# Operands of the last rows: from the rows by parts, without the normalized copy in DRAM

## The chip, the cores and the metric

One core of a Trainium2 chip. The time is the device time of one execution, in microseconds; each kernel is run several times and the median stands for it. The profile is of one further execution, taken by the hardware profiler. TensorE is called PE, VectorE DVE, ScalarE ACT, GpSimd POOL; SP issues most of the DMAs, POOL the rest.

## The reference

A transformer block with conditioned layer norms, S = 2048 rows, D = 576, hidden size F = 4608, 32 heads of 18.

```
h = layernorm(x) * (1 + ca) + sa
x = x + ga * (softmax(q k^T / sqrt(18)) v) @ wo          # q, k, v from h @ wqkv
h = layernorm(x) * (1 + cb) + sb
x = x + gb * ((sigmoid(h @ w_gate) * (h @ w_up)) @ w_down)
```

`sa, ca, ga, sb, cb, gb` are the six parts of `silu(c) @ w_mod`. Everything is float32; the kernel multiplies in a reduced float32 (`F32R`) and carries a high and a low part of each operand, so that a product is three matmuls.

## The kernel before

The gated unit (the last line of the reference) is done in two halves of 1024 rows. For each half, the hidden size is worked through in 18 blocks of 256 columns. In a block the two products with `w_gate` and `w_up` are made by a scheme with seven products in place of eight (`ORDER` names them 1, 6, 2, 7, 5, 4, 3): operands and weights are cut in two by rows and columns, and sums and differences of the pieces are multiplied. `product` (the matmuls of L1031) does one of the seven, `gate` the sigmoid and the split into high and low parts `hh` and `hl`, and `down` (L1067) the product with `w_down` for four tiles of 128 rows, added to `Oa` by DVE at L1071. `down` runs twice a block, behind products 6 and 7 of the next block. It takes PSUM banks named `d`, of which there are three.

`weights_operand` prepares the weights of a product three products ahead (`LOOK`): sums `S` on POOL (L879), the high part `w` by a cast on ACT (L913), the low parts on DVE and POOL (L918). In the first half each is also stored in DRAM (`ws`) for the second.

The seven operands of the rows lie in DRAM (`xs`), high and low parts, and are loaded into SBUF for a half as a whole. Those of the first 1024 rows are made during attention. Those of the last 1024 rows are made during the first half of the gated unit, by the generator `last_rows`: the main loop calls one of its steps at every second product. Its three stages before the change:

- Eight steps with matmuls finish the attention's output projection for each tile of 128 rows and store the row tile in DRAM (`x1d`, L1156).
- For each of two groups of four tiles, the rows are loaded again (`z<-x1d`), their mean and variance taken (`ln_stats`), normalized (`ln_rows`, L686), and `ln_spill` transposes them on PE (L701), applies scale and bias on ACT while leaving PSUM (L1160) and stores them in DRAM (`hs`, L705).
- For each third `i` of the columns four blocks `B` are loaded from `hs` (L1190), and `operand_parts` makes the seven operands from them: differences of blocks on POOL (L728); then, for each of the seven, the high part by a cast on ACT (L717), the low part by a subtraction on POOL (L719; for the last third two narrow ones, L724), and a store to `xs` (L720, L725). High and low part share a tile `ho`, of which there are two.

In `operand_parts` the casts come in a fixed order: block 11, block 22, block 21, then block 22 again once POOL has taken block 12 from it, then the three others. A cast therefore waits for POOL, and the next use of a `ho` tile for the store of its last contents.

PE's order is written out by the program from the ninth block on (`ORDERED`). The order on the other engines and on SP's queue is set by a scheduler when the kernel is built, from its own estimates of durations. Each engine works strictly in its order.

Of the kernel before, what the change touches and what calls it, by code (L numbers as in the profile page):

```python
# [23 lines left out]
P = 128  # L24
S = 2048
# [26 lines left out]
def tile_block(ctx, tc, x_in, wqkv, wo, w_gate, w_up, w_down, c_in, w_mod, out):  # L52
# [95 lines left out]
    def ln_stats(pool, xt, mv):  # L148
        st = pool.tile([P, 2, nc.vector.BN_STATS_DIM], F32, name="st", bufs=2)
        for g in range(2):  # L150
            nc.vector.bn_stats(st[:, g, :], xt[:, g, :] if len(xt.shape) == 3 else xt[:, g * HALF : (g + 1) * HALF])
        nc.vector.bn_aggr(mv, st)

    def ln_scales(pool, mv, rs):
        for _ in ln_scales_steps(pool, mv, rs):
            pass
# [72 lines left out]
        return got  # L229

    gates = dram.tile([2, D], F32, name="gates")
    hs = dram.tile([2, 3, P, S], F32, name="hs")
    x1d = dram.tile([P, 8, D], F32, name="x1d")
    x1p = dram.tile([P, 8, D], F32, name="x1p")
    oend = dram.tile([P, 8, D - DL], F32, name="oend")
# [444 lines left out]
        if t >= 8:  # L680
            nc.gpsimd.dma_start(x1p[:, t - 8, :], xt)

    def ln_rows(z, t, x1, eng):

        zx = z[:, :, 0:HALF]
        eng.tensor_scalar(  # L686
            zx, x1, mv2[:, t, 0:1], rs2[:, t : t + 1], op0=ALU.subtract, op1=ALU.mult
        )
        nc.gpsimd.tensor_copy(
            z[:, :, HALF:384].rearrange("p g (r c) -> p g r c", c=32),  # L690
            z[:, :, HALF - 32 : HALF].unsqueeze(2).to_broadcast([P, 2, 3, 32]),
        )

    def ln_spill(zs, ch, psum, pool, put):


        for g in range(2):
            for i in range(3):
                pt = psum()
                for j, z in enumerate(zs):  # L700
                    nc.tensor.transpose(pt[:, j * P : (j + 1) * P], z[:, g, i * P : (i + 1) * P], ident)  # L701
                ev = pool.tile([P, 512], F32, name="ev", bufs=2)
                c = 3 * g + i
                put(ev, pt, mcol2[:, 0, c : c + 1], mcol2[:, 1, c : c + 1])
                nc.sync.dma_start(hs[g, i, :, ch * 512 : (ch + 1) * 512], ev)  # L705
                yield

    def operand_parts(half, i, blocks, parts, hi, lo_eng, queue):


# [166 lines left out]
    def put(eng, to, a, b, op):  # L877
        for v in range(2):
            eng.tensor_tensor(to[:, v], a[:, v], b[:, v], op=op)  # L879
# [233 lines left out]
    def last_rows():  # L1113


        def psum():
            return pd.tile([P, 512], F32, name="d")

        with tc.tile_pool(name="fin", bufs=1, side="right") as pool:
            w = pool.tile([P, 2, 2, D], F32R, name="w")  # L1120
            nc.gpsimd.dma_start(w, wod)
            for t0 in (0, 4):
                od = pool.tile([P, 4, 256], F32, name="od")
                nc.sync.dma_start(od[:, :, 0:192], oend[:, t0 : t0 + 4, :])
# [12 lines left out]
                om = pool.tile([P, 512], F32R, name="om")  # L1137
                omh = pool.tile([P, 512], F32R, name="omh")
                nc.vector.tensor_copy(om[0:64], pt[0:64])
                nc.vector.tensor_copy(omh[64:P], pt[64:P])  # L1140
                nc.vector.tensor_sub(om[64:P], pt[64:P], omh[64:P].bitcast(F32))
                yield
                for j in range(4):
                    rows = slice(j * P, (j + 1) * P)
                    xt = pool.tile([P, D], F32, name="xt", bufs=2)
                    nc.sync.dma_start(xt, x1p[:, t0 + j, :])
                    for h in range(2):
                        cols = slice(h * HALF, (h + 1) * HALF)
# [10 lines left out]
        def modulated(ev, pt, scale, bias):  # L1159
            nc.scalar.activation(ev, pt, AF.Identity, scale=scale, bias=bias)  # L1160

        with tc.tile_pool(name="zp2", bufs=1, side="right") as zp:
            for ch in (2, 3):
                zs = []
                for t in range(4 * ch, 4 * ch + 4):
                    z = zp.tile([P, 2, 384], F32, name="z", bufs=4)
                    x1 = z[:, :, 0:HALF]
                    for g in range(2):
                        nc.sync.dma_start(z[:, g, 0:HALF], x1d[:, t - 8, g * HALF : (g + 1) * HALF])
                    ln_stats(zp, x1, mv2[:, t, :])  # L1170
                    zs.append(z)
                four = slice(4 * ch, 4 * ch + 4)
                ln_scales(zp, mv2[:, four, :], rs2[:, four])
                for j, z in enumerate(zs):
# [3 lines left out]
        with tc.tile_pool(name="xop2", bufs=2) as pool:  # L1178

            def get():  # L1180
                return [pool.tile([P, 512], F32, name="B", bufs=5) for _ in range(5)]

            def parts():
                return pool.tile([P, 2, 512], F32R, name="ho")

            for i in range(3):
                blocks = get()
                for (g, r), t in zip(((0, 0), (0, 1), (1, 0), (1, 1)), blocks):
                    cols = slice(HW + r * 512, HW + (r + 1) * 512)
# [96 lines left out]
```

## Time and profile before

| | |
|---|---|
| median of 3 runs | 2920.76 us (2920.69 to 2922.99) |
| the profiled execution | 2920.71 us |
| its span, first to last instruction | 2918.9 us |
| PE busy | 2855.8 us, 98% of the span |
| DVE, ACT, POOL busy | 73%, 55%, 28% |
| the chain that ended last, by engine | PE 89%, DMA 3%, ACT 3%, DVE 2%, POOL 2% |

How the lines are read. A line of a group is: source line, engine, operation, output<-inputs, partitions x elements and type, count, then busy time and mean ns of one, then the engine's idle time just before them and who ended most of it. A line of the timeline begins with the start and the length in microseconds, and ends, where the engine was idle before, with that idle time and who ended it. In a line on waits, `ACT ho L717 <- DMA xs<-ho: 39.9, 12, 6.7` says that ACT, before the instruction of L717 that writes `ho`, waited 39.9 us in 12 cases, the longest 6.7, for a DMA from `ho` to `xs`. The granted clock is a share of PE's full speed.

### The profile page before, as it was taken

The page shows a single profiled execution, that of the slowest core. Times are in us where ns is not written, and L with a number is a line of the kernel's source. Part 1 is how long each engine was busy: PE and PEld are TensorE (multiplying, and loading weights), DVE is VectorE, ACT ScalarE, POOL GpSimd, SP SyncE. Part 2 cuts the span into 40 slices and gives each one's busy share as a digit, 9 for nine tenths or more (in the row PEclk, how much of TensorE's full clock was granted, in tenths as well). Part 3 has the DMA queues.
Part 4 walks back from the last instruction along what each step waited for, and adds up shares of the span by engine and source line. Part 5 has one row for each costly group of instructions (what it writes and reads, how often), then busy time and mean ns, then how long its engine had stood idle before and what let it go on. Part 6 is the DMA issues. An engine that isn't in the chain of part 4 may idle for free.

```text
span 2918.9 us, 46640 instructions
## 1 busy us (share of the span) xinstructions
PE 2855.8 (98%) x17141; PEld 1880.8 (64%) x17141; DVE 2135.0 (73%) x3896; ACT 1614.4 (55%) x3022; POOL 814.1 (28%) x972
## 2 busy tenths in 40 slices
PE   7999999999999999999999999988999999999999
PEld 5874333343334443443443888877888888888888
DVE  7567888888888888998882777756777555555555
ACT  3227889999998888999888333333333111111111
POOL 3102014444213111661103544467543100000000
PEclk9999999999999999999999999999999999999999
DMA  5344123333212110221125866676666844444443
GB/s 176 115 147 145 49 76 131 122 125 123 90 49 77 34 53 21 99 95 63 50 86 185 289 220 234 232 250 237 225 211 238 300 167 169 167 168 167 159 159 137
DMA packets 137261, 425.97 MB, mean 146 GB/s; under 512 B 18884, under 2 KB 56520, under 8 KB 124744
## 3 DMA queue, kind: packets, MB, share of 16 engines
q1 hardware_dynamic: 121272, 342.42, 34.7%
q0 software_dynamic: 15760, 80.56, 7.8%
q8 instruction: 135, 2.21, 0.3%
q14 instruction: 94, 0.77, 0.1%
HBM read 264.45 MB, written 157.95 MB: 145 GB/s over the span
## 4 chain that ended last, share of the span: by engine, by line
PE 89%; DMA 3%; ACT 3%; DVE 2%; POOL 2%; issue 1%; SPq 1%; POOLq 0%; ACTq 0%; DVEq 0%
PE o L537 17%; PE x L1031 14%; PE d L1067 14%; PE s L959 13%; PE s L446 11%; PE bg L1031 5%; PE bu L1031 5%; PE s L294 3%; PE s L334 2%; PE s L676 2%; ACT p L963 2%; DMA xs<-ho 1%; DMA B<-hs 1%; PE s L561 1%; ACT oT L551 1%
## 5 line engine op out<-in xcount | busy, mean ns | idle before, releaser
L963 ACT ACTIVATE p<-s 128x512 f32<-128x512 f32 x2048 | 1068.5, 608 | 141.2 <-PE s L446 91.8
L459 DVE TENSOR_REDUCE mx<-s 128x1 f32<-128x512 f32 x1568 | 1015.4, 685 | 142.2 <-PE s L446 128.2
L446 PE MATMUL s<-k,q 54*128 54x512 f32 x1920 | 649.2, 439 | 2.1 <-ACT p L963 1.6
L959 PE MATMUL s<-q,k 56*128 56x512 f32 x1920 | 578.5, 433 | 2.7
L959 PEld LDWEIGHTS s<-q,k 56*128 56x128 f32 x1920 | 274.5, 185 | 472.2 <-ACT p L963 304.0
L537 PE MATMUL o<-p,vaug 128*32 128x512 f32 x4096 | 555.0, 607 | 0.0
L1067 PE MATMUL d<-wd,hh 128*128 128x288 f32 x2304 | 469.4, 298 | 20.9 <-DVE Oa L1071 20.7
L1067 PEld LDWEIGHTS d<-wd,hh 128*128 128x128 f32 x2304 | 379.0, 191 | 29.9 <-DVE Oa L1071 24.4
L1071 DVE TENSOR_TENSOR Oa<-Oa,d 128x288 f32<-128x288 f32 x576 | 257.8, 452 | 151.4 <-PE d L1067 147.8
L446 PEld LDWEIGHTS s<-k,q 54*128 54x128 f32 x1920 | 308.1, 185 | 69.2 <-ACT p L963 38.5
L1067 PE MATMUL d<-wd,hl 128*128 128x288 f32 x1152 | 343.7, 298 | 0.1
L1031 PE MATMUL x<-k,w 128*128 128x512 f32 x994 | 238.3, 390 | 0.5 <-DVE u L1245 0.5
L1043 ACT ACTIVATE u<-u 128x512 f32<-128x512 f32 x72 | 45.5, 632 | 328.9 <-DVE u L1233 310.3
L1067 PEld LDWEIGHTS d<-wd,hl 128*128 128x128 f32 x1152 | 219.7, 191 | 0.3 <-DVE hl L1047 0.3
L1031 PEld LDWEIGHTS x<-k,w 128*128 128x128 f32 x994 | 184.1, 188 | 37.5 <-DVE u L1245 0.9
L537 PEld LDWEIGHTS o<-p,vaug 128*32 128x32 f32 x4096 | 83.5, 108 | 164.7 <-issue 149.2
L1040 ACT ACTIVATE sg<-x 128x512 f32<-128x512 f32 x36 | 21.5, 598 | 285.1 <-PE x L1031 285.1
L1073 POOL DMA_DIRECT2D out_dram<-Oa x16 | 8.7, 544 | 606.4 <-DVE Oa L1071 606.4
L454 DVE CUSTOM_DVE_ANT_0 rise<-s,rise 128x512 f32<-128x512 f32 x240 | 163.4, 681 | 0.0
L452 ACT ACTIVATE rise<-s 128x512 f32<-128x512 f32 x240 | 151.4, 631 | 0.0
L918 POOL TENSOR_TENSOR w<-S,w 64x256 fp32r<-64x256 f32 x69 | 72.2, 1046 | 212.9 <-ACT w L913 202.4
L1031 PE MATMUL x<-w,w 128*128 128x512 f32 x504 | 123.5, 395 | 0.0
(240 smaller groups left out, 3772.7 us busy)
## 6 DMA issues: line engine op xcount, KB each, us to landing
w<-ws SPq DMA_DIRECT2D x126, 640.0 KB
ws<-w SPq DMA_DIRECT2D x124, 640.0 KB
wd<-wds SPq DMA_DIRECT2D x36, 1152.0 KB
wds<-w POOLq DMA_DIRECT2D x18, 1152.0 KB, 4.5
k<-kd SPq DMA_DIRECT2D x30, 360.0 KB
w<-in_B_w_down_dram POOLq DMA_DIRECT2D x18, 576.0 KB, 5.0
q<-qd SPq DMA_DIRECT2D x64, 144.0 KB
raw<-in_B_w_gate_dram SPq DMA_DIRECT2D x34, 256.0 KB
```

The lines of the kernel that those rows point to most:

```text
L294: nc.tensor.matmul(acc, w, hT[:, t, cols], start=n == 0, stop=n == len(ts_) - 1)
L446: nc.tensor.matmul(sp, qs[rows, qt * P : (qt + 1) * P], ks[rows, kc * 512 : (kc + 1) * 512], start=True, stop=True,)
L452: nc.scalar.activation(rise, sp, AF.Relu)
L454: nc.vector.tensor_tensor_reduce(rise, sp, rise, 1.0, -3.0e38, ALU.add, ALU.max, mx[0][:, qt, 0:1])
L459: nc.vector.tensor_reduce(mx[h][:, qt, j : j + 1], sp, axis=AX.X, op=ALU.max)
L537: nc.tensor.matmul(acc[32 * j : 32 * j + 32, :], vaug[:, kt, (2 * p + h) * VW : (2 * p + h) * VW + 32], probs[2 * c + h], start=kt == 0, s ...
L918: eng.tensor_sub(w[rows, :, to, :], src[rows, :, a, :], w[rows, :, a, :].bitcast(F32))
L959: nc.tensor.matmul(sT, ks[rows, kcols], qs[rows, c * 512 : (c + 1) * 512], start=True, stop=True)
L963: state["exp"] = nc.scalar.activation(pr, sT, AF.Exp, scale=SCALE)
L1031: nc.tensor.matmul(acc[v], w[:, v, a, :], X[s][:, b, :], start=first and n == 0, stop=n == 6, skip_group_check=not first,)
L1067: nc.tensor.matmul(acc[:, :HALF], a[:, f, rows], w[:, f, cols], start=n == 0, stop=n == 5)
L1071: nc.vector.tensor_add(Oa[:, t, cols], Oa[:, t, cols], acc[:, :HALF])
```

## The change

The copy `hs` in DRAM, `ln_rows` and `ln_spill` are removed. The statistics are taken from each row tile while it is still in SBUF, in the first stage. Then, for each of twelve parts (a third `i` of the columns, half `g` of them, four row tiles `r`), the 128 columns of four row tiles are loaded from `x1d` in one DMA (for the last third 32 columns), two parts ahead; DVE normalizes them, four pieces of 128x128; PE transposes them; and ACT applies scale and bias on leaving PSUM, straight into a block `B`. After four parts `operand_parts` runs on the blocks as before. Its stores are issued by POOL instead of SP, and `ho` has three tiles instead of two.

```
-    hs = dram.tile([2, 3, P, S], F32, name="hs")
...
                     nc.sync.dma_start(x1d[:, t0 + j, :], xt)
+                    ln_stats(pool, xt, mv2[:, 8 + t0 + j, :])
                     yield
...
-                    for g in range(2):
-                        nc.sync.dma_start(z[:, g, 0:HALF], x1d[:, t - 8, g * HALF : (g + 1) * HALF])
-                    ln_stats(zp, x1, mv2[:, t, :])
...
-                    ln_rows(z, 4 * ch + j, z[:, :, 0:HALF], nc.vector)
-                yield
-                yield from ln_spill(zs, ch, psum, zp, modulated)
...
-                return pool.tile([P, 2, 512], F32R, name="ho")
...
-                    nc.sync.dma_start(t, hs[g, i, :, cols])
-                yield from operand_parts(1, i, blocks, parts, nc.scalar.copy, nc.gpsimd, nc.sync)
+        with tc.tile_pool(name="xop2", bufs=1, side="right") as pool:
+            order = [(i, g, r) for i in range(3) for g in range(2) for r in range(2)]
+
+            def load_part(i, g, r):
+                z = pool.tile([P, 4, P], F32, name="z", bufs=4)
+                c0, n = g * HALF + i * P, P if i < 2 else 32
+                nc.sync.dma_start(z[:, :, 0:n], x1d[:, 4 * r : 4 * r + 4, c0 : c0 + n])
+                return z
+
+            def normalized_part(z, i, g, r):
+                to = z if i < 2 else pool.tile([P, 4, P], F32, name="z", bufs=4)
+                for j in range(4):
+                    t = 8 + 4 * r + j
...
+                    nc.vector.tensor_scalar(
+                        a, x, mv2[:, t, 0:1], rs2[:, t : t + 1], op0=ALU.subtract, op1=ALU.mult
+                    )
+                return to
+
+            def parts():
+                return pool.tile([P, 2, 512], F32R, name="ho", bufs=3)
+
+            ahead = [load_part(*order[0])]
+            for _ in ln_scales_steps(pool, mv2[:, 8:16, :], rs2[:, 8:16]):
                 yield
...
+            for n, (i, g, r) in enumerate(order):
+                pt = psum()
+                for j in range(4):
+                    nc.tensor.transpose(pt[:, j * P : (j + 1) * P], z[:, j, :], ident)
+                c = 3 * g + i
+                blocks.append(pool.tile([P, 512], F32, name="B", bufs=5))
+                nc.scalar.activation(
+                    blocks[-1], pt, AF.Identity,
+                    scale=mcol2[:, 0, c : c + 1], bias=mcol2[:, 1, c : c + 1],
+                )
+                if n + 2 < len(order):
+                    ahead.append(load_part(*order[n + 2]))
+                if n + 1 < len(order):
+                    z = normalized_part(ahead.pop(0), *order[n + 1])
+                yield
+                if g and r:
+                    blocks.append(pool.tile([P, 512], F32, name="B", bufs=5))
+                    yield from operand_parts(1, i, blocks, parts, nc.scalar.copy, nc.gpsimd, nc.gpsimd)
+                    blocks = []
```

How it moves instructions. The names are the program's; `w<-raw` and `w<-S` are the weights' casts, `sg` the first sigmoid of a block, `hh` the high part of a gate's result, `p` a copy of the first product. Lines of the changed kernel that stand for lines of the one before: L691 for L717 (the operand casts), L693 and L698 for L719 and L724, L694 and L699 for L720 and L725, L702 for L728, L887 for L913, L892 for L918, L853 for L879, L1014 for L1040, L1020 for L1046, L1173 for L1160.

On ACT, where the first set of operand casts began before:

```order
L913 CAST w<-S_23872 128x2x384
L913 CAST w<-raw_23590 128x2x384
L717 CAST ho<-B 128x512 x3
L1040 ACTIVATE sg<-x 128x512
L913 CAST w<-S_23873 128x2x384
L717 CAST ho<-B 128x512
L1046 CAST hh_24099<-sg 128x512
L717 CAST ho<-B 128x512
L913 CAST w<-raw_23882 128x2x384
L717 CAST ho<-B 128x512
```

On ACT with the change, the first set from the fourth part's eviction on:

```order
L1173 ACTIVATE B<-d,mcol_74 128x512
L1020 CAST hh_22990<-u_23031 128x512
L691 CAST ho<-B 128x512 x2
L1017 ACTIVATE p_22865<-p_22865 128x512
L887 CAST w<-raw_22844 128x2x384
L1020 CAST hh_22988<-p_22865 128x512
L691 CAST ho<-B 128x512
L1017 ACTIVATE u_22902<-u_22902 128x512
L887 CAST w<-S_23208 128x2x384
L691 CAST ho<-B 128x512
L1205 COPY p_23236<-x 128x512
L1020 CAST hh_22990<-u_22902 128x512
```

and the third set, likewise:

```order
L1173 ACTIVATE B<-d,mcol_74 128x512
L1020 CAST hh_25107<-u_25019 128x512
L691 CAST ho<-B 128x512
L1205 COPY p_25354<-x 128x512
L691 CAST ho<-B 128x512
L1205 COPY p_25354<-x 128x512
L887 CAST w<-S_25258 128x2x384
L691 CAST ho<-B 128x512
L887 CAST w<-raw_24960 128x2x384
L691 CAST ho<-B 128x512 x3
L1014 ACTIVATE sg<-x 128x512
```

In the first set before, three casts of the six shown stand ahead of `sg`, behind the block's last `w<-raw`. With the change one cast of each set stands about a block earlier, and the six others between the fourth part's eviction and the next `sg`: in the first set all of them ahead of the last `w<-raw`, in the third set three ahead of it and three right behind. The three sets begin with their evictions in blocks 4, 7 and 11 (counted from 0) and end in blocks 6, 9 and 12.

On POOL, the last third before (the narrow subtractions):

```order
L724 TENSOR_TENSOR ho<-B,ho 32x512 x2
L918 TENSOR_TENSOR w<-S_24576,w 64x2x128
L879 TENSOR_TENSOR S_24925<-S_24924,raw_24585 128x384 x2
L728 TENSOR_TENSOR B<-B 128x512
L918 TENSOR_TENSOR w<-raw_24585,w 64x2x128
L728 TENSOR_TENSOR B<-B 128x512
L724 TENSOR_TENSOR ho<-B,ho 32x512 x2
L728 TENSOR_TENSOR B<-B 128x512
L724 TENSOR_TENSOR ho<-B,ho 32x512 x2
```

and with the change:

```order
L702 TENSOR_TENSOR B<-B 128x512
L853 TENSOR_TENSOR S_25671<-raw_25268 128x384
L702 TENSOR_TENSOR B<-B 128x512
L698 TENSOR_TENSOR ho<-B,ho 32x512 x3
L699 DMA xs<-ho 128x512
L702 TENSOR_TENSOR B<-B 128x512
L892 TENSOR_TENSOR w<-S_25258,w 64x2x128
L698 TENSOR_TENSOR ho<-B,ho 32x512
L853 TENSOR_TENSOR S_25604<-raw_25268,raw_25333 128x384 x2
L699 DMA xs<-ho 128x512
L853 TENSOR_TENSOR S_25671<-raw_25268 128x384
L892 TENSOR_TENSOR w<-raw_24960,w 64x2x128
```

The store's issue now stands on POOL between them, and the third difference (the one on which the fourth cast depends) behind three narrow subtractions and an issue.

More of the change, by code (lines that the diff above doesn't have):

```diff
@@ L681, in project_o @@
             nc.gpsimd.dma_start(x1p[:, t - 8, :], xt)
[L683 to L694, printed above, removed]
-        for g in range(2):
[L698 to L705, printed above, removed]
-                yield
     def operand_parts(half, i, blocks, parts, hi, lo_eng, queue):
@@ L1156, in last_rows @@
                     nc.sync.dma_start(x1d[:, t0 + j, :], xt)
+                    ln_stats(pool, xt, mv2[:, 8 + t0 + j, :])
                     yield
[L1159 to L1168, printed above, removed]
-                        nc.sync.dma_start(z[:, g, 0:HALF], x1d[:, t - 8, g * HALF : (g + 1) * HALF])
-                    ln_stats(zp, x1, mv2[:, t, :])
[L1171 to L1174, printed above, removed]
-                    ln_rows(z, 4 * ch + j, z[:, :, 0:HALF], nc.vector)
-                yield
-                yield from ln_spill(zs, ch, psum, zp, modulated)
@@ L1178, in last_rows @@
[L1178 to L1183, printed above, removed]
-                return pool.tile([P, 2, 512], F32R, name="ho")
[L1186 to L1189, printed above, removed]
-                    nc.sync.dma_start(t, hs[g, i, :, cols])
-                yield from operand_parts(1, i, blocks, parts, nc.scalar.copy, nc.gpsimd, nc.sync)
+        with tc.tile_pool(name="xop2", bufs=1, side="right") as pool:
[9 more added lines that the diff above has]
+                    t = 8 + 4 * r + j
+                    if i < 2:
+                        a, x = z[:, j, :], z[:, j, :]
+                    else:
+                        a = to[:, j, :].rearrange("p (n c) -> p n c", c=32)
+                        x = z[:, j, 0:32].unsqueeze(1).to_broadcast([P, 4, 32])
+                    nc.vector.tensor_scalar(
[6 more added lines that the diff above has]
+            for _ in ln_scales_steps(pool, mv2[:, 8:16, :], rs2[:, 8:16]):
+                yield
+            ahead.append(load_part(*order[1]))
+            yield
+            z = normalized_part(ahead.pop(0), *order[0])
+            blocks = []
[13 more added lines that the diff above has]
+                    z = normalized_part(ahead.pop(0), *order[n + 1])
+                yield
+                if g and r:
+                    blocks.append(pool.tile([P, 512], F32, name="B", bufs=5))
+                    yield from operand_parts(1, i, blocks, parts, nc.scalar.copy, nc.gpsimd, nc.gpsimd)
+                    blocks = []
```

## The prediction

> **What bounds the kernel now.** I read the page's busy times first, then the chain of waits in order of time, then TensorE's instructions where that chain leaves it.
>
> ```profile
> span 2918.9 us, 46640 instructions
> PE 2855.8 (98%) x17141; PEld 1880.8 (64%) x17141; DVE 2135.0 (73%) x3896; ACT 1614.4 (55%) x3022; POOL 814.1 (28%) x972
> ```
>
> PE is the bound: only what makes it wait or work can move the time. The change lies in the first half of the gated unit. There PE's own rows show each block's third product (seven products and two down steps make a block):
>
> ```profile
> 1903.99 3.35 PE L1031 MATMUL x<-w,w 128*128 128x512 f32 x14
> 1946.29 3.35 PE L1031 MATMUL x<-w,w 128*128 128x512 f32 x14
> 1995.43 3.35 PE L1031 MATMUL x<-w,w 128*128 128x512 f32 x14
> 2037.36 3.37 PE L1031 MATMUL x<-w,w 128*128 128x512 f32 x14
> 2072.37 3.35 PE L1031 MATMUL x<-w,w 128*128 128x512 f32 x14
> ```
>
> The last pair is a clean block: 35.0 us. The three blocks before it, in which the operands are built, took 133.4 where three clean ones take 105.0: **28.4 us are lost**, all of it without extra PE work. Where PE stood, its timeline says:
>
> ```profile
> 1914.14 0.53 PE L1067 MATMUL d<-wd,hh 128*128 128x288 f32 x2 [1.25 <-DVE Oa L1071]
> 1916.98 0.85 PE L1067 MATMUL d<-wd,hh 128*128 128x288 f32 x2 [1.78 <-DVE Oa L1071]
> 1960.79 0.85 PE L1067 MATMUL d<-wd,hh 128*128 128x288 f32 x2 [4.81 <-DVE Oa L1071]
> 1988.87 0.85 PE L1067 MATMUL d<-wd,hh 128*128 128x288 f32 x2 [4.70 <-DVE Oa L1071]
> 2031.68 0.64 PE L1067 MATMUL d<-wd,hh 128*128 128x288 f32 x2 [4.31 <-DVE Oa L1071]
> ```
>
> These are 16.9 us. PE waits for VectorE to empty a bank of the down product; VectorE was itself waiting for a cast on ScalarE; and ScalarE, which works in order, stood at the operand casts (the list of who waited for whom, 1690 to 2400 us: total, times, longest):
>
> ```profile
> ACT ho L717 <- DMA xs<-ho: 39.9, 12, 6.7
> ACT ho L717 <- DMA B<-hs: 18.8, 5, 6.6
> ```
>
> The other 11.5 us are the clock: after such a stall it is granted below full speed for some microseconds (0.77 in the stretch of the 4.70 stall; columns: stretch, length, PE, PEld, DVE, ACT, POOL busy, clock, DMA).
>
> ```profile
> 1980.00:1995.00 15.00, 10.24 (x52) 9.54 (x51) 9.54 (x16) 6.74 (x12) 11.78 (x11) 0.77 0.65 241
> ```
>
> **The change, part by part.** PE's work is the same: 48 transposes go and 48 come, in the same banks. The 12 evictions with scale and bias stay on ScalarE. Gone: 12 stores to and 12 loads from the DRAM copy, the wait for those loads (18.8 us of ScalarE's time), two table loads on ScalarE, eight 0.60 us copies on POOL. VectorE gets 48 pieces of 128x128 for 8 rows of 128x576; the 589 ns row bounds them above and the 199 ns of an almost empty VectorE instruction below; at 0.25 us it is 12 for 4.7 us over nine blocks, of which about 0.3 us stands before a bank's emptying in each set: under 1 us on the path.
>
> ```profile
> L689 POOL COPY z<-z 128x192 f32<-128x192 f32 x8 | 4.6, 602 | 14.8 <-DMA raw<-in_B_w_gate_dram 7.6 <-DVE z L686 7.0
> L686 DVE TENSOR_SCALAR z<-z,mv,rs 128x576 f32<-128x576 f32 x8 | 4.2, 589 | 0.1
> L152 DVE BATCH_NORM_AGGREGATE mv<-st 128x2 f32<-128x12 f32 x8 | 1.6, 199 | 0.0
> ```
>
> The loads of parts are two steps ahead, some 20 us before their transposes, so I cost them at nothing; without that cover each would stop PE for its landing.
>
> The 21 operand stores move from SP's queue to POOL's, and their tile has three buffers for two. On POOL such an issue costs 0.73 us (0.56 for a narrow one) and lands 3.2 to 5.2 us later; I take 4.0:
>
> ```profile
> L720 POOL DMA_DIRECT2D xs<-t x9: 727/727/807, 1176.2 to 1262.3; - x9
> L725 POOL DMA_DIRECT2D xs<-t x5: 543/560/633, 1291.0 to 1326.5; - x5
> xs<-t POOLq DMA_DIRECT2D x9, 512.0 KB, 3.2
> Oa<-x1d POOLq DMA_DIRECT2D x8, 288.0 KB, 5.2
> ```
>
> What decides is the order. Before, the 21 casts stand spread over five blocks. Now they stand in three sets: cast 1 early, casts 2 to 7 close together (in the third set all six ahead of the next `sg`). Cast 4 needs a subtraction on POOL that stands behind all earlier POOL work, and casts 5, 6 and 7 reuse the buffers of 2, 3 and 4, so they need those stores landed. POOL's prices:
>
> ```profile
> L719 POOL TENSOR_TENSOR ho<-B,ho 128x512 fp32r<-128x512 f32 x14 | 18.9, 1350 | 14.0 <-ACT ho L717 13.7
> L724 POOL TENSOR_TENSOR ho<-B,ho 32x512 fp32r<-32x512 f32 x14 | 19.7, 1407 | 1.6 <-ACT ho L717 0.7
> L728 POOL TENSOR_TENSOR B<-B 128x512 f32<-128x512 f32 x12 | 16.3, 1355 | 7.6 <-DMA B<-hs 7.0
> L879 POOL TENSOR_TENSOR S<-raw 128x384 f32<-128x384 f32 x28 | 35.8, 1299 | 12.7 <-DVE w L918 12.6
> L918 POOL TENSOR_TENSOR w<-S,w 64x256 fp32r<-64x256 f32 x60 | 62.1, 1035 | 191.0 <-ACT w L913 181.0 <-issue 7.5 <-POOL ho L719 0.5
> ```
>
> I lay each set over the clean block of the trace (ScalarE's and VectorE's rows of it):
>
> ```profile
> 2094.28 0.62 ACT L1046 CAST hh<-p 128x512 fp32r<-128x512 f32 x1 [1.17 <-DVE p L1044]
> 2096.57 0.82 ACT L913 CAST w<-S 128x768 fp32r<-128x768 f32 x1
> 2098.03 0.62 ACT L1046 CAST hh<-u 128x512 fp32r<-128x512 f32 x1 [0.64 <-DVE u L1044]
> 2101.24 0.84 ACT L913 CAST w<-raw 128x768 fp32r<-128x768 f32 x1 [0.89 <-POOL S L879]
> 2102.29 0.44 DVE L1071 TENSOR_TENSOR Oa<-Oa,d 128x288 f32<-128x288 f32 x1
> 2103.34 0.81 DVE L1071 TENSOR_TENSOR Oa<-Oa,d 128x288 f32<-128x288 f32 x2
> 2109.16 0.60 ACT L1040 ACTIVATE sg<-x 128x512 f32<-128x512 f32 x1 [7.08 <-PE x L1031]
> 2114.70 0.46 DVE L1071 TENSOR_TENSOR Oa<-Oa,d 128x288 f32<-128x288 f32 x1
> ```
>
> VectorE's second `Oa` stands behind the weights' subtraction, which needs the `w<-raw` cast; the `Oa` at 2114.70 stands behind `sg`. Whatever makes these casts late makes PE late, less about 0.6 us that the three banks cover.
>
> *Third set* (narrow parts). The fourth block is there at 2098.6. POOL then does subtraction, S, subtraction, three narrow ones, an issue, the subtraction for cast 4: 3 x 1.36 + 1.30 + 3 x 1.41 + 0.56 = 10.2, so cast 4 starts at 2108.8 and `w<-raw` at 2109.4, eight late. Up to the store that cast 7 needs, POOL has another w, narrow, S, S, issue, S, w, subtraction, three narrow, issue: 2 x 1.0 + 4 x 1.41 + 3 x 1.25 + 1.36 + 2 x 0.56 = 13.9, to 2122.7; landed at 2126.7; `sg` then starts at 2127.3 instead of 2109.2. Its product, the two weights' and `hl` pieces and two adds (3.9 us on VectorE) put the `Oa` at about 2131.7 instead of 2114.7: 17.0, less 0.6: **16.4 us**.
>
> *First set.* Fourth block at 2090.6 on POOL; subtraction twice, S, operand, S, issue, w, subtraction: 9.5; cast 4 at 2100.1 where ScalarE was free at 2096. Cast 6 waits for a store issued at 2102.2 (landed 2106.2), cast 7 for one issued at 2108.0 (2112.0). `w<-raw` ends at 2113.5, the second `Oa` at 2114.7 instead of 2103.8: 10.9, less 0.6: **10.3**.
>
> *Second set.* From 2094.9 on POOL: two subtractions, an operand, an issue (2099.7, landed 2103.7: cast 5), w, a subtraction (2102.1: cast 4), an operand, an issue (2104.2, landed 2108.2: cast 6). `w<-raw` ends at 2109.7, the second `Oa` at 2110.9: 7.1, less 0.6: **6.5**.
>
> Together 33.2 us of stalls. They make four stretches of reduced clock where now there are five for 11.5 us: 9.2. So 42.4 us are lost where 28.4 are now: **+14.0**, and 2920.7 (the profiled execution; span 2918.9; median of the three runs 2920.8) becomes 2934.7, less some tenths for the freed SP queue and table loads: **2934**.
>
> The bounds. For all stores out of an operand tile the trace has
>
> ```profile
> DMA to landing us min/median/max: 2.3/3.8/7.3
> ```
>
> that is 1.7 less or 3.3 more than my 4.0, in each of three sets: minus 5 and plus 10. POOL 6% quicker (1.27 in place of 1.35): minus 4.5. So 2925 to 2944 for this case alone.
>
> The Trainium skill (TensorE: Matmul & The Clock Gate, "What's actually happening") says that about 3.4 us of idleness halves the clock, for about 3.4 us. Here a stall of 1.78 us, soon after one of 1.25, was already followed by a pair of 0.85 us where the pair before took 0.53: the trace does not agree on the threshold. By the rule the clock term would be an estimated 6.8 us, and the time 2932.
>
> **The rivals.**
>
> *Faster: the waits fall into ScalarE's idle.* Now 58.7 us of cast waits cost PE only 16.9, 29%: ScalarE is idle for 7.1 us ahead of `sg`, and several waits lie there. By the sums above the new sets wait about 42 us; at 29% this is 12, with 8 of clock 20: 28.4 - 20 = 8 us gained, 2912. All gone: 2892. For it: SP's queue no longer stands between a cast and its store. Against it: the new order puts the casts ahead of the casts that VectorE needs. 22%.
>
> *No change*: short landings and quick POOL work bring the loss down to today's 28 us: 2921. 14%.
>
> *Slower still: POOL's issues stretch.* If each issue took twice its 0.73 us beside a busy VectorE, the four to five that stand on each set's path add about 3 us a set: 2944. The issues in this stage took 0.53 to 0.57, which speaks against it. 8%. The Trainium skill (SBUF — State Buffer, "Who interferes with whom") names the mechanism: VectorE in a two-port mode locks POOL out of writing descriptors. No issue of this kind stands in the stage before, so the trace cannot decide it.
>
> *The change does not do what it says*: PE stops at a transpose because a part is late. One load stood on the chain before:
>
> ```profile
> 1826.06 3.52 DMA z<-x1d
> ```
>
> A late part would cost PE about these 3.5 us, from the point where its load is issued under 4 us ahead of its transposes; SP's order puts it further. With my own case: 2938, 3%.
>
> **How the numbers follow.** My own case has 53%, slower still 8%, late parts 3%, no change 14%, faster 22%. Two tenths of a per cent, about what a measurement of this kernel can tell from no change, are 5.8 us: slower, 64%; same, 14%; faster, 22%. The range holds my case (2925 to 2944), the stretched issues and most of the faster rival down to 2908: 2908 to 2946, leaving about 10% below and 6% above.
>
> **What would show it.** Right: ScalarE's idle before the operand casts is about 40 us, now ended by the stores and by POOL's subtraction, none by a load; POOL is busy 14 of 15 us in three places, each about a block long and three blocks apart; PE's waits for `Oa` gather there, the longest in the third set; blocks between the sets take 35.0 us. Wrong: PE's waits for `Oa` in all three sets together under 17 us (then the casts are not late when VectorE needs them), or a wait of PE at a transpose, or blocks in which POOL is idle and PE still waits.

## The result

The changed kernel takes 2943.45 us (median of six, 2941.07 to 2949.19) where the kernel before, on the same chip, takes 2920.73. The ratio is 1.0081, interval 1.0068 to 1.0094: **slower by about 23 us**. 2934 had been forecast, with 2908 to 2946 as the range. The forecast was right in its sign and its range, but the experiments below show that its main term was not what made the difference.

The page of the changed kernel (the profiled execution is the slowest of the six, 2949.19 us):

```profile
span 2947.4 us, 46594 instructions
PE 2866.2 (97%) x17141; PEld 1888.6 (64%) x17141; DVE 2154.8 (73%) x3930; ACT 1610.9 (55%) x3019; POOL 819.3 (28%) x985
```

Its span is 28.5 us longer, but 6.4 of these lie ahead of the stage: the first product shown starts at 1722.88 for 1716.52. Kernels that are the same up to there put it between 1714.8 and 1723.2, so I compare the stage itself, 13 blocks from that product on. Busy time of each engine in it, then the granted clock and the DMAs' share (columns: stretch, length, PE, PEld, DVE, ACT, POOL, clock, DMA, GB/s). Before:

```profile
1716.52:2212.29 495.77, 476.20 (x2602) 420.89 (x2601) 354.77 (x583) 173.71 (x260) 271.88 (x243) 0.98 0.67 231
```

and with the change:

```profile
1722.88:2239.01 516.13, 480.66 (x2602) 425.32 (x2601) 372.09 (x602) 170.13 (x257) 279.38 (x256) 0.97 0.61 209
```

The stage is 20.4 us longer for the same matmuls. PE's idle time in it (length less busy) went from 19.6 to 35.5, that is 15.9; the other 4.5 are PE's rows growing longer at a lower clock. VectorE is busy 17.3 us more, in a stage in which it was already the busiest after PE. PE's own stalls, from its timeline:

```profile
1774.08 0.53 PE L1041 MATMUL d<-wd,hh 128*128 128x288 f32 x2 [1.83 <-DVE Oa L1045]
1801.79 0.58 PE L1041 MATMUL d<-wd,hh 128*128 128x288 f32 x2 [2.64 <-DVE Oa L1045]
1837.24 3.35 PE L1005 MATMUL x<-k,w 128*128 128x512 f32 x7 [4.70 <-DVE u L1239]
1851.17 0.54 PE L1041 MATMUL d<-wd,hh 128*128 128x288 f32 x2 [2.96 <-DVE Oa L1045]
1964.33 0.85 PE L1041 MATMUL d<-wd,hh 128*128 128x288 f32 x2 [6.66 <-DVE Oa L1045]
2041.57 0.85 PE L1041 MATMUL d<-wd,hh 128*128 128x288 f32 x2 [4.25 <-DVE Oa L1045]
2087.46 0.85 PE L1041 MATMUL d<-wd,hh 128*128 128x288 f32 x2 [7.13 <-DVE Oa L1045]
2106.46 0.85 PE L1041 MATMUL d<-wd,hh 128*128 128x288 f32 x2 [4.66 <-DVE Oa L1045]
```

Five of them (4.70, 2.96, 6.66, 7.13, 4.66: 26.1 us) lie where the operand casts stand gathered. Three (1.83, 2.64, 4.25: 8.7 us) do not: two come ahead of the first set, one at the very first cast of the third. The forecast knows nothing of these three. The granted clock is 0.50 in seven stretches of this stage, 34.1 us together, of which PE is busy for 28.4; before, in four stretches, 20.5 us together (17.5 busy). At half speed half of this busy time is lost, an estimated 14.2 us with the change and 8.8 before. Three of the seven stretches, 4.9 us of the loss, follow the three stalls outside the sets.

**The sets.** The group of ScalarE's operand casts, 1690 to 2130 us, with the idle time ahead of them and who ended it:

```profile
L691 ACT CAST ho<-B 128x512 fp32r<-128x512 f32 x21 | 12.8, 619 | 36.7 <-DMA xs<-ho 13.1 <-POOL B L702 10.8 <-POOL S L853 5.4
```

and the third set on ScalarE's timeline:

```profile
2084.38 0.62 ACT L691 CAST ho<-B 128x512 fp32r<-128x512 f32 x1 [7.91 <-POOL B L702]
2091.21 0.62 ACT L691 CAST ho<-B 128x512 fp32r<-128x512 f32 x1 [4.96 <-POOL w L892]
2100.19 0.62 ACT L691 CAST ho<-B 128x512 fp32r<-128x512 f32 x1 [8.36 <-DMA xs<-ho]
2100.72 0.59 ACT L1014 ACTIVATE sg<-x 128x512 f32<-128x512 f32 x1
```

These are casts 4, 6 and 7. Cast 4 waits for POOL's difference, cast 6 for POOL (by the order, a store stuck behind its work), cast 7 for a store, and `sg` stands behind them. The fourth block was there at 2073.1: `sg` starts 27.6 us later, where the replay by hand had 28.7.

**VectorE's pieces.** The 48 normalized pieces of 128x128, as a group over the same stretch, and six places of the timelines:

```profile
L1152 DVE TENSOR_SCALAR z<-z,mv,rs 128x128 f32<-128x128 f32 x48 | 28.1, 612 | 5.8 <-DMA z<-x1d 5.6
...
1761.41 0.60 DVE L1152 TENSOR_SCALAR z<-z,mv,rs 128x128 f32<-128x128 f32 x2
1770.58 0.35 DVE L1152 TENSOR_SCALAR z<-z,mv,rs 128x128 f32<-128x128 f32 x1 [3.08 <-DMA z<-x1d]
1774.01 1.21 POOL L892 TENSOR_TENSOR w<-raw,w 64x256 fp32r<-64x256 f32 x1
1774.92 0.39 DVE L1152 TENSOR_SCALAR z<-z,mv,rs 128x128 f32<-128x128 f32 x1
1794.07 2.32 POOL L853 TENSOR_TENSOR S<-raw 128x384 f32<-128x384 f32 x2 [0.68 <-POOL w L892]
1794.46 2.01 DVE L1152 TENSOR_SCALAR z<-z,mv,rs 128x128 f32<-128x128 f32 x2
1838.76 1.29 POOL L702 TENSOR_TENSOR B<-B 128x512 f32<-128x512 f32 x1
1838.79 1.35 DVE L1152 TENSOR_SCALAR z<-z,mv,rs 128x128 f32<-128x128 f32 x1
2032.58 2.31 POOL L853 TENSOR_TENSOR S<-raw 128x384 f32<-128x384 f32 x2 [0.68 <-DVE w L892]
2032.97 4.82 DVE L1152 TENSOR_SCALAR z<-z,mv,rs 128x128 f32<-128x128 f32 x6
```

At 1761 POOL is idle and two pieces take 0.60 us. At 1794 POOL works on two sums `S` and a piece takes 1.0; at 2033 it works on two sums, a `w` and a narrow subtraction, and six pieces take 0.8 each on average. The ends of the rows show what a piece waits for. The one of 1838.79 ends at 1840.14, POOL's difference beside it at 1840.05; the one of 1774.92 ends at 1775.31, POOL's `w` at 1775.22. Of the 48 pieces 23 end 0.08 to 0.09 us after the end of an instruction on POOL, and these took 0.39 to 1.44 us; the other 25 took 0.33 to 0.36. So a piece that meets a running `tensor_tensor` of POOL, of whatever line, is done only when that is through. At 1770 VectorE stands for 3.08 us, because a part has not landed; what is behind it on VectorE is the emptying of PE's banks.

### The profile page after: what moved, and what is told of

It is laid out like the page before. It is cut to its first block, busy times and chain, and to the rows that moved or that the text cites. A ratio compares the mean times of both kernels' runs of the same rounds, so it can differ in the third digit from the quotient of the medians.

```text
span 2947.4 us, 46594 instructions
## 1 busy us (share of the span) xinstructions
PE 2866.2 (97%) x17141; PEld 1888.6 (64%) x17141; DVE 2154.8 (73%) x3930; ACT 1610.9 (55%) x3019; POOL 819.3 (28%) x985
## 4 chain that ended last, share of the span: by engine, by line
PE 88%; DVE 4%; ACT 3%; DMA 2%; issue 2%; POOL 2%; SPq 0%; POOLq 0%; DVEq 0%; ACTq 0%
PE o L536 17%; PE d L1041 15%; PE x L1005 14%; PE s L933 13%; PE s L445 10%; PE bg L1005 5%; PE bu L1005 5%; PE s L293 3%; PE s L333 2%; PE s L675 2%; ACT p L937 1%; DVE w L892 1%; PE s L560 1%; ACT oT L550 1%; DMA ws<-w 0%
## 5 line engine op out<-in xcount | busy, mean ns | idle before, releaser
L1041 PEld LDWEIGHTS d<-wd,hh 128*128 128x128 f32 x2304 | 382.0, 192 | 41.2 <-DVE Oa L1045 35.4
L1014 ACT ACTIVATE sg<-x 128x512 f32<-128x512 f32 x36 | 21.5, 598 | 315.9 <-PE x L1005 315.9
L892 POOL TENSOR_TENSOR w<-S,w 64x256 fp32r<-64x256 f32 x69 | 69.0, 1000 | 251.8 <-ACT w L887 247.3
```

The lines of the kernel that those rows point to most:

```text
L892: eng.tensor_sub(w[rows, :, to, :], src[rows, :, a, :], w[rows, :, a, :].bitcast(F32))
L1041: nc.tensor.matmul(acc[:, :HALF], a[:, f, rows], w[:, f, cols], start=n == 0, stop=n == 5)
```

## The experiments

The theories. **A**: ScalarE stands at gathered operand casts (the prediction). **B**: VectorE's pieces, held up beside POOL, and its waiting for parts. **C**: POOL's issues themselves. **D**: the amount of operand work, wherever it stands. **E**: something else in the change. Ratios are to the kernel before, timed on the same chip; "stage" is the length of the 13 blocks in the profiled execution.

| kernel | median us | ratio (95% interval) | stage us |
|---|---|---|---|
| before | 2920.7 to 2923.5 | 1 | 495.8 |
| the change | 2943.45 | 1.0081 (1.0068 to 1.0094) | 516.1 |
| 1 change, stores on SP | 2934.95 | 1.0034 (1.0022 to 1.0047) | 505.1 |
| 2 change, casts on POOL | 2941.05 | 1.0056 (1.0044 to 1.0068) | 511.0 |
| 3 change, pieces on ScalarE | 2932.43 | 1.0031 (1.0019 to 1.0043) | 507.2 |
| 4 before, stores on POOL, three `ho` | 2947.86 | 1.0083 (1.0071 to 1.0095) | 519.8 |
| 5 change, casts spread | 2924.54 | 1.0000 (0.9991 to 1.0009) | 493.4 |
| 6 as 5, stores on SP | 2921.29 | 0.9995 (0.9986 to 1.0003) | 495.3 |
| 7 as 5, pieces on ScalarE | 2916.65 | 0.9977 (0.9967 to 0.9988) | 488.2 |
| 8 before, casts spread | 2903.77 | 0.9933 (0.9920 to 0.9946) | 478.6 |
| 9 change, no pieces | 2933.32 | 1.0037 (1.0024 to 1.0050) | 502.3 |
| 10 as 5, no pieces | 2910.89 | 0.9962 (0.9949 to 0.9975) | 481.6 |
| 11 as 5, parts four ahead | 2917.35 | 0.9985 (0.9972 to 0.9997) | 488.2 |
| 12 as 7, parts four ahead | 2916.64 | 0.9977 (0.9968 to 0.9985) | 487.6 |

### 1. Stores back on SP

```
- yield from operand_parts(1, i, blocks, parts, nc.scalar.copy, nc.gpsimd, nc.gpsimd)
+ yield from operand_parts(1, i, blocks, parts, nc.scalar.copy, nc.gpsimd, nc.sync)
```

> The changed kernel with its operand stores issued by SP again; three tiles `ho` as in the change, ScalarE's order all but the same. Theory A (ScalarE stands at the operand casts, waiting for POOL's subtractions and for stores, and VectorE and PE follow): POOL's path to cast 4 and to the store of cast 7 loses one and four to five issues of 0.56 to 0.73 us, under 3 us a set, but the stores now wait in SP's order behind the weights' stores; casts' waits for stores grow from 13 us to 20 or more, and the time stays at 2938 to 2950. Theory C (POOL's issues are the loss): 2930 or below, casts waiting less than 25 us in all. Theory B (the loss is VectorE's normalization, held up beside POOL): no change from the issues, 2940 to 2946, and PE's waits of 1.8, 2.6 and 4.3 us outside the sets' middle remain.

2934.95 us, 8.5 less than the change: between A's figure and C's. The casts' waits on ScalarE are the same in sum (list of waits, 1700 to 2150 us: total, times, longest):

```profile
ACT ho L691 <- DMA xs<-ho: 18.8, 5, 8.4
ACT ho L691 <- POOL B L702: 16.7, 3, 7.4
```

35.5 us for 36.7, but PE's stall of 2.96 us is gone, 6.66 became 4.4 in two pieces and 4.66 became 0.78. POOL without issues reaches some of its differences sooner, and SP did not make the stores as late as A had it. So issuing on POOL costs something where casts stand gathered, and neither theory sized it. Kernels 5 and 6 show that it costs nothing that can be measured where they don't.

### 2. Casts on POOL

```
- ..., parts, nc.scalar.copy, nc.gpsimd, nc.gpsimd)
+ ..., parts, nc.gpsimd.tensor_copy, nc.gpsimd, nc.gpsimd)
```

> The changed kernel with the 21 operand casts on POOL instead of ScalarE; nothing on ScalarE waits for a store or for POOL's differences any more, and the order of all other instructions is nearly unchanged. Theory A: the PE waits of the three sets (4.7, 3.0, 6.7, 7.1, 4.7: 26 us) and their reduced clock (about 8 us) go, 2943 becomes 2909 to 2920, the higher end if POOL's 21 more instructions of about 1 us hold up the weights' sums. Theory B: the waits stay, 2938 or more, because they come from VectorE's pieces. Theory C: POOL has as many issues and more work, so no gain, 2943 or more.

2941.05 us. A's 2909 to 2920 failed plainly. No cast waits on ScalarE now, but POOL's chain is longer, and PE found a new wait in the third set:

```profile
2032.81 0.85 PE L1041 MATMUL d<-wd,hh 128*128 128x288 f32 x2 [5.51 <-DVE Oa L1045]
...
2103.99 3.78 PE L1005 MATMUL x<-big,w 128*128 128x512 f32 x8 [6.33 <-POOL w L892]
```

The second row is PE waiting for weights whose low part is late on POOL. Taking the casts from one in-order engine to another moved the wait. The first row is one of the three stalls outside the sets, and it has stayed.

### 3. Pieces on ScalarE

```
- nc.vector.tensor_scalar(a, x, mv2[:, t, 0:1], rs2[:, t : t + 1], op0=ALU.subtract, op1=ALU.mult)
+ nc.scalar.activation(a, x, AF.Identity, scale=rs2[:, t : t + 1], bias=nb[:, t - 8 : t - 7])
```

(`nb` is minus mean times `rs`, two instructions on VectorE.)

> The changed kernel with the 48 pieces of 128x128 normalized on ScalarE (scale and bias by row) instead of VectorE. Theory A: the sets remain (ScalarE still stands at casts) and ScalarE gets some 14 us more work, 2940 to 2950. Theory B: the pieces that took up to 1.4 us on VectorE beside POOL, and VectorE's 5.6 us of waiting for loaded parts, are what delays VectorE: PE's waits of 1.8 and 2.6 us (first parts) and 4.3 us (first cast of the third set) vanish and 2943 falls by these 8.7 us and some 3 of clock, to about 2932, or further if the sets too were VectorE's.

2932.43 us, B's figure, though B's places only in part. On ScalarE a piece takes the same time whatever POOL does:

```profile
L1152 ACT ACTIVATE z<-z,nb,rs x48: 477/484/508, 1754.7 to 2027.3; 128x128 f32<-128x128 f32 x48
```

(min/median/max ns, where VectorE had 329/352/1442.) Of the three stalls outside the sets 2.64 became 0.53 and 0.94, and 4.25 became 0.97; 1.83 stayed as 2.12, behind a late part. So 4.6 of these 8.7 us remain. The rest of the gain lies inside the sets, whose stops fell from 26.1 to 22.4 us although the casts were not touched; the longest is 7.13 us as before.

### 4. Queue and buffers alone, on the kernel before

```
- return pool.tile([P, 2, 512], F32R, name="ho")
+ return pool.tile([P, 2, 512], F32R, name="ho", bufs=3)
- yield from operand_parts(1, i, blocks, parts, nc.scalar.copy, nc.gpsimd, nc.sync)
+ yield from operand_parts(1, i, blocks, parts, nc.scalar.copy, nc.gpsimd, nc.gpsimd)
```

> The kernel before, with two parts of the change alone: the operand stores issued by POOL, and three tiles `ho`. The copy in DRAM and its loads stay. Theory A: the loss depends on where the casts stand and what they wait for; stores land about 4 us after POOL's subtraction instead of waiting in SP's order, so the 39.9 us of cast waits on stores fall to 15 to 25, while the order draws the first casts closer: 2912 to 2925. Theory C (issuing on POOL costs): 2930 or above. Theory B: no normalization by pieces here, so as before, 2921 give or take what the stores bring.

2947.86 us: 24 us slower, the opposite of what A expected, though by A's own mechanism. With these two edits the scheduler draws all 21 casts into about two blocks, and they wait more than in either kernel:

```profile
ACT ho L717 <- DMA xs<-ho: 38.7, 8, 8.0
...
ACT ho L717 <- POOL B L728: 20.4, 3, 9.2
...
ACT ho L717 <- DMA B<-hs: 18.3, 4, 7.3
...
PE x L1031 <- DVE u L1245: 14.4, 1, 14.4
```

77 us, and a single stop of PE of 14.4. My expectation had misjudged how far the order would move. C expected 2930 or above, so this kernel alone does not tell A from C; 5 and 6 do.

### 5 and 6. Casts spread

```
+ turn[0] = nc.scalar.copy(st["hh", r][:, f, :], t)      # in gate
...
+ def late_copy(out, in_):
+     with tc.issue_after(turn[0].ins):                  # on ScalarE: behind the last hh cast
+         nc.scalar.copy(out, in_)
...
- ..., parts, nc.scalar.copy, nc.gpsimd, nc.gpsimd)
+ ..., parts, late_copy, nc.gpsimd, nc.gpsimd)           # 6: nc.sync for the last
```

> The changed kernel with one thing added: each operand cast is queued on ScalarE behind the last `hh` cast that the program has written by then, so that the 21 casts stand about 10 us apart over two blocks each, instead of six within 20 us. Work, queues and buffers are those of the change. Theory A (the loss is that the casts stand gathered: each then waits for POOL or a store, and ScalarE's casts for VectorE queue behind): waits ahead of operand casts fall from 36.7 us to under 8, the PE waits inside the sets (26 us) and some 6 us of clock go, those outside (1.8, 2.6, 4.3) stay: 2908 to 2918. Theory D (it is the amount: POOL's 40 operand instructions hold up VectorE and the weights wherever they stand, as the casts on POOL did): 2930 or more.

> As the spread kernel, with the operand stores on SP's queue instead of POOL's. Theory A: with 10 us between casts and three tiles no cast waits for a store on either queue, so within 3 us of the spread kernel. Theory C (an issue on POOL costs in itself): 3 to 8 us faster than the spread kernel.

2924.54 and 2921.29 us: by the medians 18.9 and 22.2 less than the change (by the ratios some 24 and 25), and no different from the kernel before. No wait ahead of an operand cast is left in the list of either kernel. So the gathered casts do cost time, though more than A's 2908 to 2918 remained. D's 2930 did not come either. The difference between POOL's queue and SP's lies inside both intervals. What still stops PE in kernel 5 is VectorE:

```profile
2016.67 3.47 DVE L1152 TENSOR_SCALAR z<-z,mv,rs 128x128 f32<-128x128 f32 x5
2024.18 0.85 PE L1041 MATMUL d<-wd,hh 128*128 128x288 f32 x2 [4.05 <-DVE Oa L1045]
```

### 8. The same order for the kernel before

The edit of 5, on the call in the kernel before (stores on SP, two `ho`).

> The kernel before with the same order for its 21 casts and nothing else: copy in DRAM, stores on SP, two tiles `ho`. Theory A: the 28.4 us that these three blocks lose now are of the same kind, cast waits fall from 58.7 us to under 20, and it becomes 2896 to 2908. Theory D: 2915 or more, since the work on POOL is the same.

2903.77 us, **0.67% faster than the kernel before**, and the fastest of all here: A's figure, where D expected 2915 or more. Its stage and its only wait for an operand cast:

```profile
1717.30:2195.86 478.56, 469.59 (x2603) 413.06 (x2601) 358.16 (x583) 172.31 (x260) 274.77 (x243) 1.00 0.70 239
...
ACT ho L1188 <- DMA B<-hs: 1.1, 1, 1.1
```

This is the result that turns the explanation. Spreading gains 0.67% on the kernel before, and 0.81% on the change. Casts at which ScalarE has to wait are a loss, but **both kernels had it**: the kernel before, too, with its casts over five blocks, waited 58.7 us at them, and 1.1 us in this order. In the same order the change is still 20.8 us slower by the medians, 14.8 in the stage.

### 9 and 10. Without the pieces

```
- c0, n = g * HALF + i * P, P if i < 2 else 32
+ c0, n = g * HALF + (i * P if i < 2 else HALF - P), P
...
  def normalized_part(z, i, g, r):
-     ... # four pieces
-     return to
+     return z
```

> The changed kernel without the 48 pieces of normalization: the parts are transposed as loaded (the last third loads 128 columns in place of 32). Left out of the computation: the normalization of the last 1024 rows ahead of the gated unit. Theory B (VectorE's pieces beside POOL, 28 us of VectorE): PE's waits of 2.6, 4.3 and most of 4.7 us go, and 2943 becomes 2924 to 2932. Theory A alone (the gathered casts are the whole surplus): 2938 or more.

> The spread kernel, likewise without the 48 pieces. Left out: the same. With the casts in the same order, the changed kernel was 2924.5 and the kernel before 2903.8. Theory B: these 20.7 us are the pieces and VectorE's standing behind late parts, so 2903 to 2910 (part of the late loads stays, as a wait of PE at the transposes). Theory E (it is something else in the change: strided loads, evictions among the operands' casts, statistics in the first stage): 2915 to 2922.

2933.32 us in the change's order (theory B expected 2924 to 2932), 2910.89 with the casts spread (2903 to 2910; E from 2915): both about 1 us above B's range. Their stages:

```profile
1716.54:2218.84 502.30, 476.20 (x2603) 421.58 (x2601) 348.21 (x554) 169.81 (x257) 280.60 (x256) 0.97 0.64 217
```

```profile
1722.69:2204.27 481.58, 471.00 (x2603) 414.73 (x2602) 355.03 (x554) 169.14 (x257) 283.42 (x256) 1.00 0.66 226
```

No stall of PE lies outside the sets in 9; inside them are 6.00, 2.55, 5.87, 7.12, 2.81 and 0.76 us, 25.1 where the change has 26.1. So taking the pieces out removes just the three stalls that the forecast did not know: PE's idle time falls by 9.4 us and its busy time, by the clock, by 4.5. PE never waits at a transpose in either.

The stages add up to a ledger of the 20.4 us. The pieces: 516.1 - 502.3 = **13.8**. The waiting casts: 502.3 - 481.6 = 20.7 in the changed kernel against 495.8 - 478.6 = 17.2 in the one before, so **3.5** more. The rest, 481.6 - 478.6: **3.0**. By the ratios, times 2922 us, the same three are 0.0044, 0.0008 (0.0075 against 0.0067) and 0.0029: 12.9, 2.3 and 8.5 us. The ratios' intervals are some 0.0025 wide, so an entry is good to some 5 us. Taken out in the other order, casts first, the stages give 11.8 for the pieces (493.4 - 481.6) and 5.5 for the casts (22.7 against 17.2). The parts are not independent: with the casts spread the pieces themselves take 23.5 us instead of 28.1, and stores on SP alone (kernel 1) already take 11.0 us off the stage. Either way the pieces come first, and the casts cost far less than 14 us more than before. What the rest is, stays open; a part may lie ahead of the stage, which the eleven kernels with the change start at 1719.5 us on average and the three without it at 1717.1.

### 7, 11 and 12. Pieces and parts with the casts spread

Kernel 7 is kernel 5 with the pieces of kernel 3, each queued behind an `hh` cast. Kernels 11 and 12 are 5 and 7 with the parts loaded four ahead for two (and two `ho`, to make room):

```
- if n + 2 < len(order):
-     ahead.append(load_part(*order[n + 2]))
+ if n + 4 < len(order):
+     ahead.append(load_part(*order[n + 4]))
```

> As the spread kernel, with the 48 pieces normalized on ScalarE, queued in the same manner behind the `hh` casts. Theories A and B together: both losses go, 2943 less 32 for the gathered casts and 11 for VectorE's pieces: 2897 to 2906, faster than both kernels, with hardly a wait of PE above 2 us in the stage. Theory D: 2922 or more.

> The spread kernel with the parts loaded four ahead instead of two (six tiles `z` for four, two tiles `ho` for three to make room). If VectorE's 5.9 us of waiting for parts reach PE (its wait of 2.1 us in the second block, and 1.9 us two blocks on): 2918 to 2922; if they are covered: 2923 to 2926. Two tiles `ho` should cost nothing at 10 us from cast to cast.

> The spread kernel with the pieces on ScalarE and the parts loaded four ahead. Pieces and late parts both taken off VectorE: 2908 to 2914 by theory B; 2916 or more if the 10 us that are left over the kernel before with spread casts have another source than late parts, ScalarE's 20 us of pieces above all.

7: 2916.65 us, 0.23% faster than before, but more than 10 us above what A and B together expected. The pieces now stand on ScalarE ahead of the weights' casts, and one of PE's stalls, 1.75 us, waits for an eviction behind them, another, 1.02 us, at a transpose for a piece. 11: 2917.35 us, by the medians 7.2 less than kernel 5, by the stage 5.2 (the intervals of the two ratios overlap). VectorE's waits for parts fell from 5.9 us to

```profile
DVE z L1152 <- DMA z<-x1d: 1.4, 2, 0.7
```

That is not what PE gained, though. Of the two stalls that the expectation named, 2.09 stayed as 1.86, and 1.93 gave way to 1.31 and 0.74, which kernel 10, without pieces, has too. What went is above all the 4.05 us at 2024, now 0.61: the eight pieces that stood there, most of them beside POOL's work, now stand before 1930 us, and the 48 take 17.8 us instead of 23.5. So kernel 11 shows mainly what the place of the pieces is worth, and does not show what late parts cost. 12: 2916.64 us, as 7, above the 2908 to 2914 that B expected: with the pieces off VectorE, loading earlier gains nothing. None of these reaches kernel 8.

## Why the prediction was right, and where it was wrong

**What bounds the kernel** held: PE is stopped by VectorE's late emptying of a bank, and VectorE by what is ahead on its own or ScalarE's order. Of the 11.5 us that were put down to the clock before the change 10.2 are so by PE's busy time (115.2 us in these three blocks where three clean ones have 105.0); the other 1.3 are further stops of PE. Spreading the casts took 17.2 of the 28.4 us that the prediction read as lost from the three blocks before the change; the rest stays with the operand work even when no cast waits (the six blocks of kernel 8 from 1905.12 to 2125.86 take 220.7 us where six clean ones take 210).

**The gathered casts** behave much as replayed, and cost less. ScalarE's waits are 36.7 us (about 40 forecast), ended by stores and by POOL, none by a load; cast 4, cast 7 and `sg` of the third set came 11.3, 27.1 and 27.6 us after the fourth block. POOL is busy for 14.3 to 14.4 of 15 us in the three sets, as forecast. The first set stopped PE for 4.70 and 2.96 us (10.3 forecast), the second for 6.66 (6.5 forecast). The third gave 7.13 and 4.66, not 16.4 at once; the likely reason, which no run isolates, is that the first stop had already moved PE's need for `sg` back, which the replay over an undisturbed block could not see. Together these are 26.1 us for 33.2, and with 9.3 us of clock (9.2 forecast) 35.4 for 42.4. One term that was too large is the landing of a store, 4.0 us: its median was 3.2 (2.6 for narrow ones). Of the blocks between the sets two take 35.0; those in which parts are transposed or normalized take 36.1 and 41.3.

**The step that failed is the difference**: "42.4 us are lost where 28.4 are now". By kernels 5, 8, 9 and 10 the waiting casts cost about 21 us with the change and 17 without, 3.5 more and not 14. The clock was part of it: the prediction let its loss fall from 11.5 to 9.2 us, while by the granted clock it rose from 8.8 to 14.2, in seven stretches and not four. Of the 20.4 us that the stage is longer, the three stalls outside the sets make 8.7 us and 4.9 of clock: 13.6, about what the stage loses without the pieces.

**The term that was mis-sized** is VectorE's pieces: "12 for 4.7 us, under 1 us on the path". They took 28.1 us, and removing them gives 13.8 us of the stage, 12.9 by the ratios. The bound was wrong as a bound: the 589 ns row of 128x576 stood alone or beside POOL's copies, of which never more than 0.3 us was left when it began (573 to 603 ns), and a piece a quarter of that size took up to 1442 ns beside POOL's `tensor_tensor` (that one beside a subtraction for an operand). How much of the 13.8 us is this standing, how much the pieces' own time and how much late parts, no run separates. The Trainium skill (SBUF — State Buffer, "Who interferes with whom") says that `tensor_scalar` may run in a mode that takes the port pair which VectorE shares with POOL, and that whichever issues first holds it for its whole instruction while the other is blocked. The trace agrees for the pieces: 23 of 48 end 0.08 to 0.09 us after an instruction of POOL. The prediction had cited that section for POOL's issues, which did not stretch (725 to 807 ns), and had not applied it to the pieces. That the slow pieces end with POOL's instruction, and that on ScalarE they are not slow, is shown; that the ports are what the two share, no run here isolates.

**Loads "at nothing"** was not right either, by an amount that lies within those 13.8 us and that no run isolates. The cover of 20 us was counted to the transposes; the pieces stand a step earlier, and VectorE waited 5.6 us for parts. The rival that spoke of late parts looked for the wait at PE, and none is there in the change.

**The rivals.** Casts that wait in ScalarE's idle time: no, kernel 5 gains 18.9 us by the medians when they stop waiting. POOL's issues stretched: no.

So the time came out 9 us above the forecast, with two errors of opposite sign: about 10 us too much for the casts and some 12 too little for the pieces, with the unexplained rest on top. That the forecast had the right sign and the range held the result was in good part luck.

## What to carry to other kernels

Before a difference between two versions is put down to one loss, take that loss out of both: the waiting casts were real, worth 0.67%, and in both kernels. On an in-order engine an instruction whose operand is late should stand where what is behind it is not urgent; one order edge for each of 21 casts gained more here than any change of work. A short VectorE operation has to be priced beside what POOL does at that moment, not by a larger one beside an idle POOL, and a load ahead is to be counted to the first instruction that touches it.

## What the runs showed of the hardware that was not expected

A 128x128 float32 `tensor_scalar` on VectorE takes 0.33 to 0.36 us, beside POOL's issue of a DMA too (two in 0.61 us at 1792). If it meets a running `tensor_tensor` of POOL it ends 0.08 to 0.09 us after that one and takes up to 1.44; kernels 1, 2, 5, 6 and 11 show the same 0.08 to 0.09. On ScalarE it takes 477 to 508 ns throughout.

The granted clock after a stop of PE does not follow the stop's length alone. In these traces it is 1.00 or 0.50 and changes in steps of 3.41 us, whose borders lie on one grid through the whole stage (columns as for the stage above). The stop of 1.83 us in the changed kernel lay within one step (the first row) and was followed by a step at 0.50; the longer one of 2.96 lay across two (the third and fourth rows) and was followed by none:

```profile
1771.43:1774.84 3.41, 1.57 (x12) 1.34 (x11) 3.41 (x8) 0.00 (x0) 3.09 (x3) 1.00 0.48 192
1774.84:1778.25 3.41, 3.41 (x16) 3.28 (x15) 1.91 (x6) 0.00 (x0) 0.39 (x1) 0.50 0.64 194
1846.52:1849.94 3.42, 1.70 (x13) 1.46 (x11) 0.54 (x1) 1.35 (x2) 3.27 (x4) 1.00 0.62 237
1849.94:1853.35 3.41, 2.18 (x16) 2.18 (x17) 2.64 (x6) 0.00 (x0) 3.33 (x5) 1.00 0.49 196
1853.35:1856.76 3.41, 3.41 (x20) 3.00 (x19) 1.09 (x3) 0.48 (x1) 2.73 (x4) 1.00 0.77 263
```

Nor does the first pair behind a stop tell it: in kernel 3 the pair behind 3.77 us took 0.54 us, and the clock fell 0.9 us after its start. How much of a step has to be idle, no run here settles.

```profile
2090.59 0.54 PE L1041 MATMUL d<-wd,hh 128*128 128x288 f32 x2 [3.77 <-DVE Oa L1045]
...
2091.53:2094.94 3.41, 3.41 (x15) 3.39 (x15) 1.26 (x4) 0.00 (x0) 2.92 (x4) 0.50 0.68 268
```
